# One pinned order for the first batch of an attention and gated-MLP kernel

## The chip, the cores and the metric

The kernel runs on one core of one Trainium2 chip. The time is the device time of one launch in microseconds (us); the median of several launches counts. Five engines work side by side, each through its own queue in order: TensorE (PE, matrix products), VectorE (DVE), ScalarE (ACT), GpSimd (POOL) and SyncE (SP), which here only issues DMA transfers between device memory and the on-chip memory. Engines wait for one another by semaphores.

## The reference: what is computed

Batch 8, 8 heads, sequence 576, head size 64, all in float32. Linear attention without a softmax comes first: per head a 64x64 product of keys and values, then queries times that product, then a normalization by the root mean square over the head. Its output, 512 columns wide, goes through an MLP with a spatial gate:

```
kv  = einsum('bhsd,bhse->bhde', k, v)
out = einsum('bhsd,bhde->bhse', q, kv)
x   = out / sqrt(mean(out*out) + 1e-6) * g_norm          # heads side by side: 512 columns
h   = relu(x @ w_in)                                     # 512 x 1024
u, v = h[..., :512], h[..., 512:]
v_n = (v - mean(v)) / sqrt(var(v) + 1e-6)
v_s = einsum('ts,bsd->btd', w_spatial, v_n) + b_spatial
return (u * v_s) @ w_out                                 # 512 x 512
```

The weights `w_in` and `w_out` reach the kernel as 64-bit numbers (two 32-bit words each) and are turned into float32 on the chip.

## The kernel before, in words

The 8 heads are taken as 4 pairs of 128 rows; the 576 positions are 4 tiles of 128 and a tail of 64. The batches are worked one after the other: `first(b)` (the v half, then the u half of the first MLP product), `second(b)` (the spatial product) and `last(b)` (the output product), with the attention of later batches put between their steps. From batch 1 on these products are made of three passes of a faster number format: each operand is split in a high and a low part (`WIH`, `WIL`, `XH`, `XL` and so on).

Batch 0 is different. Its weights are still arriving, so its products are made in plain float32 from the weights as they are decoded, and the splits of the weights are made meanwhile. What is done for batch 0, with the attention of batch 1 among it, is written as a string of tokens, `PLAN`, which a loop works through (lines 720 to 721). One letter is one step:

- `N`, `n`: zero products on PE whose result nobody reads (8, then four groups of 6, 8, 6 and 6 in the plan: the `n` groups are 26 in all).
- `W` issues the next weight load, `L` the next load of attention inputs. These come per pair: keys and values `KV` (128x1024 numbers) and their tail `KT`, then the queries `qt`. There are two buffers each.
- `C` decodes one weight tile: an absolute value on ACT (line 570) and five steps on DVE (lines 571 to 575).
- `J` is the key-value product of one pair, `K` that of two (line 128), with two copies of the result (lines 145 and 146).
- `A` and `D` are the product with the queries (line 203, and 156 for the tail's part) with the squares of the norm; `B` is the end of the norm on DVE; `T` is the transpose on PE (line 231) and its copy on ACT (line 233 for batch 0, 224 and 225 for others).
- `Hck` adds pair `k` to the v half of position tile `c` (line 366); it needs the transpose of pair `k` and the decoded tile `k` of `w_in`. `e` and `F` finish the v half. `ukj` is the same for the u half (line 390). `h` is the v half of the tails (line 372), `s` one unit of the spatial product in float32 (lines 399 and 400).
- `X`, `E`, `z` and `O` split weights for the batches to come (lines 579, 580, 623 to 631 and 319); `Q` decodes a tile of `w_out`; `R` splits the gated result `U` for the output product.

The tokens give the order in which instructions are recorded. A scheduler then puts each engine's instructions in an order of its own, by priorities and a model of times; only some instructions, marked by `keep_in_program_order`, stay in the recorded order among themselves. So the queue of an engine can differ from the plan. On SP a DMA also waits for the DMA eight places ahead of it, since eight semaphores go round.

Of batch 1, the loads of keys come first for all pairs and then all queries (line 634).

Of the kernel before, what the change touches and what calls it, by code (L numbers as in the profile page):

```python
# [10 lines left out]
U32 = mybir.dt.uint32  # L11
I32 = mybir.dt.int32
AF = mybir.ActivationFunctionType
ALU = mybir.AluOpType
# [3 lines left out]
DM, FF = 512, 1024  # L18
FH = FF // 2
P = 128  # L20
NP = H // 2
# [9 lines left out]
EPS = 1e-6  # L31
HALF = DM // 2
NB = B
PLAN = """
N8 W L J00 n6 D00 L n8 W G J01 n6 B00 C A01 L n6 W L J02 T00 H00 H10 D02 C H20 H30 B01 W C J03 T01 Z H01 H11 D03 H21 H31 W C
W B02 L T02 H02 H12 H22 H32 W B03 C W d0 T03 H03 H13 H23 H33 b0 e0 e1 e2 e3 C L C t0 L K10 C
u00 u01 u02 u03 F0 L F1 W W L K12 F2 W W W W d1 b1 F3 u10 Q0 u11 X0 u12 L A10 X1 u13 t1 X2 L B10 A11 h X3
T10 s L B11 E0 T11 s A12 s L B12 E1 z s T12 A13 X4 W s B13 L X5 Q1 s T13 X6 L s X7 s P O0 O1 p R W
"""


def f32(ap):
    return ap.bitcast(F32)
# [3 lines left out]
def body(ctx: ExitStack, tc, qT, kvm, kvt, g2, w_in, wsT, bsp, w_out, out):  # L47
    nc = tc.nc
# [5 lines left out]
    work = ctx.enter_context(tc.tile_pool(name="work", bufs=2))  # L54
# [23 lines left out]
    R = [vpool.tile([P, 14 * HF], F32, name=f"R{x}", tag=f"V{x}") for x in "HL"]  # L78
# [42 lines left out]
    def att_k(b, pairs, st, copy=nc.vector.tensor_copy):  # L121
        ps = ps_att.tile([P, 512], F32, name="pskv", tag="att")
        to = KVO[pairs[0] // 2] if b % 2 else KVB
        ends, first = [], None

        def product(p, of, h, c):
            at = (p - pairs[0]) * P + h
            return nc.tensor.matmul(ps[h:h + D, at:at + D], of[:, 0, h:h + D], of[:, 1, h:h + D],  # L128
                                    start=c == 0, stop=c == NC)

        for p in reversed(pairs):
            kv, kt, qs = keys.pop((b, p))
# [12 lines left out]
        copy(to[0:D, own, 0:D], both[0:D, :, 0:D])  # L145
        nc.scalar.copy(to[D:P, own, D:P], both[D:P, :, D:P])
        for p, qs in reversed(ends):
            if qs is not None:
                att_end(p, st, qs)
        issue()  # L150

    def att_end(p, st, q):

        if p == 0:
            st["tail"] = ps_tail.tile([P, 512], F32, name="pst", tag="tail")
        nc.tensor.matmul(st["tail"][:, p * P:(p + 1) * P], q, st[p], start=True, stop=True)  # L156
# [42 lines left out]
    def att_qa(b, p, st, accumulate=False):  # L199
        qt = queries.pop((b, p))  # L200
        ps = ps_att.tile([P, 512], F32, name="pso", tag="att")
        for c in range(NC):
            nc.tensor.matmul(ps[:, c * P:(c + 1) * P], qt[:, c * P:(c + 1) * P], st[p],  # L203
                             start=True, stop=True)
        if b % 2 == 0:
            att_end(p, st, qt[:, S - P:S])
        issue()
        st[p] = norm_a(ps, P, accumulate)
# [330 lines left out]
    staged, decoded, psu = {}, {}, {}  # L539
# [20 lines left out]
    def load_out(k):  # L560
        load64(w_out[k * P:(k + 1) * P, :], 2 * NP + k, stage0 if k == 1 else stage2)

    def weight64(i):

        wide = staged.pop(i).rearrange("p (f two) -> p f two", two=2)
        w0, w1 = wide[:, :, 0], wide[:, :, 1]
        to = W32[i] if i < 2 * NP else f32(w1)
        t = work.tile([P, DM], U32, name="t", tag="stg", bufs=2)
        keep = tc.keep_in_program_order if i in (2 * NP, 2 * NP + 1) else lambda ins: ins
        keep(nc.scalar.activation(f32(t), f32(w1), AF.Abs, scale=2.0 ** -112))  # L570
        keep(nc.vector.tensor_scalar(t, t, 3, None, op0=ALU.logical_shift_left))
        nc.vector.scalar_tensor_tensor(w1, w1, 0x80000000, t, op0=ALU.bitwise_and, op1=ALU.bitwise_or)
        nc.vector.tensor_scalar(t, w1, 0xFF800000, None, op0=ALU.bitwise_and)
        nc.vector.scalar_tensor_tensor(f32(w0), w0, 2.0 ** -52, f32(t), op0=ALU.mult, op1=ALU.mult)
        nc.vector.tensor_tensor(to, f32(w1), f32(w0), op=ALU.add)
        return to
# [7 lines left out]
        split_w(WIH[:, n % NP, fs], WIL[:, n % NP, fs], W32[n])  # L584

    def make_out(k):
        decoded[k] = weight64(2 * NP + k)

    def split_out(k):
        split(WOH[:, k, :], WOL[:, k, :], decoded.pop(k))  # L590
# [41 lines left out]

    todo = [(0, p, "f") for p in range(NP)]
    for b in range(1, B):
        kinds = ("k", range(NP)), ("q", range(NP))
        if b % 2 == 0:
            kinds = [(kind, ps) for ps in ((0, 1), (2, 3)) for kind in "eq"]
        todo += [(b, p, kind) for kind, ps in kinds for p in ps]
    states = {}
    wanted = [0]  # L640
# [7 lines left out]
    def ahead(n=1):  # L648
        wanted[0] += n
        issue()  # L650
# [11 lines left out]
    def warm(n):  # L662

        ps = ps_tail.tile([P, 512], F32, name="psw", tag="tail")
        for _ in range(n):
            nc.tensor.matmul(ps[:, 0:P], KVB[:, 1], KVB[:, 1], start=True, stop=True)

    def filler(n):
        for _ in range(n):
# [5 lines left out]
    def enqueue(b, late=0):  # L675
        if b < NB:
            queue.extend(att_steps(b)[late])
# [12 lines left out]
    def outw():  # L690
# [5 lines left out]
    loads = [lambda k=k: load_in(1, k) for k in range(NP)]  # L696
    loads += [lambda k=k: load_in(0, k) for k in range(NP)]
    loads += [lambda c=c: load_ws(c) for c in range(NC)] + [load_tail]
    loads += [lambda k=k: load_out(k) for k in range(NP)]
    makes = list(range(2 * NP))  # L700
    units = [(d, j) for d in range(4) for j in range(2)]

    psv = [ps_mm.tile([P, 512], F32, name="psh", tag="mm") for _ in range(NC)]
    st = [states.setdefault(b, {}) for b in range(2)]
    do = {
        "N": warm, "n": filler,
        "L": lambda: ahead(), "W": lambda: loads.pop(0)(), "C": lambda: weight64(makes.pop(0)),
        "K": lambda b, p: att_k(b, (p, p + 1), st[b]), "A": lambda b, p: att_qa(b, p, st[b]),
        "B": lambda b, p: att_qb(b, p, st[b]), "T": lambda b, p: att_t(b, p, st[b]),
        "J": lambda b, p: att_k(b, (p,), st[b], nc.scalar.copy),  # L710
        "D": lambda b, p: att_qa(b, p, st[b], True), "d": lambda b: tail_a(b, st[b], True),
        "a": lambda b: tail_a(b, st[b]), "b": lambda b: tail_b(b, st[b]),
        "t": lambda b: att_tail(b, st[b]),
# [3 lines left out]
        "s": lambda: sp_32(*units.pop(0)), "X": split_in, "E": split_ws, "z": split_tail,  # L717
        "Z": blank_tails, "P": outw, "p": gates, "Q": make_out, "O": split_out, "R": split_g,
    }
    for token in PLAN.split():  # L720
        do[token[0]](*map(int, token[1:]))

    ahead(len(todo))
    VH, VL = (vpool.tile([P, 2, 7, HF], F32R, name=f"V{x}", tag=f"V{x}") for x in "HL")
# [35 lines left out]
    last(1)  # L760
    for b in range(2, NB):
        first(b)
# [50 lines left out]
```

## Time and profile before

| | us |
|---|---|
| median of 3 runs (lowest, highest) | 522.61 (522.24, 522.8) |
| the profiled execution's own time | 521.54 |
| its span, first to last instruction | 519.7 |
| PE busy | 507.7 (98% of the span) |
| DVE busy | 360.0 (69%) |
| ACT busy | 240.1 (46%) |

The span is read from the first to the last instruction of the profiled execution. A busy PE is one with a matmul in flight. A float32 matmul of the program counts as two in the trace's numbers (x8 for four steps). The DMA engines are busy all the time from 8 to 29 us (share 1.02), and at 0.82 from there to 40 us; after that they have room.

### The profile page before, as it was taken

What the parts mean: (1) busy time and instruction counts of PE and PEld (TensorE: products, weight loads), DVE (VectorE), ACT (ScalarE), POOL (GpSimd) and SP (SyncE); (2) the same over time, 40 slices, a digit from 0 to 9 for tenths busy, and PEclk for the clock granted to TensorE, in tenths of its full rate; (3) what the DMA queues carried; (4) which work ended last, traced back from release to release, by engine and by line L of the source; (5) the groups of instructions that cost most, each with busy time, mean ns of one, the idle gap of its engine ahead of it and who ended that gap; (6) DMA issues with size and microseconds to landing.
All of it is one profiled execution on the core that took longest, in us unless ns stands there. A gap on an engine that the chain in (4) does not pass through costs nothing.

```text
span 519.7 us, 9439 instructions
## 1 busy us (share of the span) xinstructions
PE 507.7 (98%) x3548; PEld 450.0 (87%) x3548; DVE 360.0 (69%) x1075; ACT 240.1 (46%) x615; POOL 8.5 (2%) x23
## 2 busy tenths in 40 slices
PE   7889999999999999999999999999999999999996
PEld 7647878798998899889998899989998899988995
DVE  3987498998781788648593598918785388938470
ACT  3554565674533464335343356325443355434321
POOL 5000000000000000000000000000000000000000
PEclk9999999999999999999999999999999999999999
DMA  8985110333326002111425401230233201020003
GB/s 267 346 309 170 56 45 23 93 126 90 124 96 197 12 2 64 41 65 53 139 79 172 133 22 33 75 133 3 76 101 133 73 1 34 9 82 0 1 1 101
DMA packets 22304, 46.50 MB, mean 89 GB/s; under 512 B 2866, under 2 KB 7474, under 8 KB 22260
## 3 DMA queue, kind: packets, MB, share of 16 engines
q1 hardware_dynamic: 22260, 45.91, 27.3%
q8 instruction: 28, 0.46, 0.3%
q14 instruction: 16, 0.13, 0.1%
HBM read 36.46 MB, written 9.44 MB: 88 GB/s over the span
## 4 chain that ended last, share of the span: by engine, by line
PE 86%; DMA 5%; DVE 4%; ACT 3%; issue 1%; SPq 0%; DVEq 0%
PE pso L283 19%; PE psu L283 17%; PE psh L316 13%; PE psb L422 6%; PE pso L203 4%; PE psc L422 4%; PE psa L422 4%; PE pskv L128 4%; DMA KV<-kvm 3%; PE psu L390 3%; PE pstr L231 2%; PE psh L366 2%; PE psh L283 2%; PE pst L156 1%; DMA KT<-kvt 1%; DVE WSL L580 1%
## 5 line engine op out<-in xcount | busy, mean ns | idle before, releaser
L283 PE MATMUL psu<-XH,WIH 128*128 128x288 f32 x224 | 66.5, 297 | 0.0
L283 PE MATMUL psu<-XL,WIH 128*128 128x288 f32 x224 | 66.1, 295 | 0.0
L283 PE MATMUL psu<-XH,WIL 128*128 128x288 f32 x224 | 66.0, 295 | 0.0
L283 PE MATMUL pso<-WOH,GH 128*128 128x512 f32 x144 | 57.1, 398 | 0.0
L283 PE MATMUL pso<-WOL,GH 128*128 128x512 f32 x144 | 56.7, 394 | 0.0
L283 PE MATMUL pso<-WOH,GL 128*128 128x512 f32 x144 | 54.0, 396 | 0.0
L449 ACT CAST GH<-g 128x288 fp32r<-128x288 f32 (+2 forms) x84 | 26.7, 350 | 47.9 <-DVE g L441 47.5
L295 DVE BATCH_NORM_STATS2 s<-v 128x6 f32<-128x512 f32 x32 | 22.0, 691 | 36.2 <-ACT v L289 36.1
L316 PE MATMUL psh<-WIH,XH 128*128 128x512 f32 x112 | 44.3, 396 | 0.0
L316 PE MATMUL psh<-WIL,XH 128*128 128x512 f32 x112 | 43.7, 390 | 0.0
L316 PE MATMUL psh<-WIH,XL 128*128 128x512 f32 x112 | 43.0, 391 | 0.1
L283 PEld LDWEIGHTS psu<-XH,WIH 128*128 128x128 f32 x224 | 42.0, 188 | 0.4
L283 PEld LDWEIGHTS psu<-XL,WIH 128*128 128x128 f32 x224 | 42.0, 188 | 0.3
L283 PEld LDWEIGHTS psu<-XH,WIL 128*128 128x128 f32 x224 | 42.0, 188 | 0.0
L320 DVE TENSOR_TENSOR VL<-v,VH 128x512 fp32r<-128x512 f32 (+1 forms) x56 | 33.8, 621 | 7.9 <-ACT VH L319 7.6
L523 ACT COPY o<-pso 128x512 f32<-128x512 f32 x35 | 19.7, 588 | 39.6 <-PE pso L283 28.6
L190 DVE TENSOR_REDUCE ss<-x 128x8 f32<-128x512 f32 x35 | 23.8, 681 | 19.1 <-ACT x L189 19.0
L413 ACT ACTIVATE U<-psu 128x288 f32<-128x288 f32 x56 | 22.9, 412 | 28.5 <-PE psu L283 27.5
L319 ACT CAST VH<-v 128x512 fp32r<-128x512 f32 (+1 forms) x56 | 30.4, 564 | 10.8 <-DVE v L342 7.0
L283 PEld LDWEIGHTS pso<-WOH,GL 128*128 128x128 f32 x144 | 27.0, 188 | 5.7
L283 PEld LDWEIGHTS pso<-WOL,GH 128*128 128x128 f32 x144 | 27.1, 188 | 5.0
L283 PEld LDWEIGHTS pso<-WOH,GH 128*128 128x128 f32 x144 | 27.1, 188 | 4.7
(187 smaller groups left out, 1219.1 us busy)
## 6 DMA issues: line engine op xcount, KB each, us to landing
KV<-kvm SPq DMA_DIRECT2D x31, 512.0 KB, 4.4
out<-o SPq DMA_DIRECT2D x32, 256.0 KB, 2.1
qt<-qT SPq DMA_DIRECT2D x16, 288.0 KB, 2.9
stage<-w_in SPq DMA_DIRECT2D x8, 512.0 KB, 9.0
qt<-qT SPq DMA_DIRECT2D x16, 256.0 KB, 2.7
KT<-kvt SPq DMA_DIRECT2D x32, 64.0 KB, 4.1
stage<-w_out SPq DMA_DIRECT2D x4, 512.0 KB, 4.4
stage<-wsT SPq DMA_DIRECT2D x4, 288.0 KB, 5.2
```

What stands on the lines that cost most here:

```text
L128: return nc.tensor.matmul(ps[h:h + D, at:at + D], of[:, 0, h:h + D], of[:, 1, h:h + D], start=c == 0, stop=c == NC)
L190: nc.vector.tensor_reduce(ss, heads(x), axis=AX.X, op=ALU.add)
L203: nc.tensor.matmul(ps[:, c * P:(c + 1) * P], qt[:, c * P:(c + 1) * P], st[p], start=True, stop=True)
L283: nc.tensor.matmul(ps, lt, rh, start=i == 0, stop=i == n - 1)
L295: nc.vector.bn_stats(s6, v)
L316: nc.tensor.matmul(ps, lt, rh, start=k == 0 and i == 0, stop=k == NP - 1 and i == 2)
L319: nc.scalar.copy(hi, x)
L320: nc.vector.tensor_tensor(lo, x, f32(hi), op=ALU.subtract)
L413: nc.scalar.activation(U[:, d, cols], ps[:, 0:HS], AF.Relu)
L422: nc.tensor.matmul(ps, lt, rh, start=start and i == 0, stop=stop and i == len(pairs) - 1, skip_group_check=True)
L449: nc.scalar.copy(GH[:, d, dst], g[:, src])
L523: nc.scalar.copy(o, ps)
```

## The change

The plan is written anew. Three kinds of marks are in it: a stretch in brackets is pinned, which means that its instructions on PE, ACT and SP keep their recorded order (DVE's don't); a bar makes everything recorded after it stand behind the last DVE instruction recorded before it; and a new letter `c` is the first half of a decode (ACT's absolute value), with `C` the rest on DVE. 6 zero products of the 26 are left. The copies of `K` are both on ACT. The loads of batch 1 come in two halves: keys of two pairs, their queries, then the other two. The two decodes of `w_out` in the plan are pinned as well.

```diff
-N8 W L J00 n6 D00 L n8 W G J01 n6 B00 C A01 L n6 W L J02 T00 H00 H10 D02 C H20 H30 B01 W C J03 T01 Z H01 H11 D03 H21 H31 W C
...
+[ W N8 G L c W C J00 L A00 c C L L n6 W J01 A01 J02 B00 T00 | W D02 B01 c H00 H20 J03 H30 T01 A03 C B02 W H31
+W c T02 c c H21 H10 W H22 H11 H32 C B03 c C H01 W T03 H02 | H12 H33 c H03 L H13 H23 e0 L L W C C L a0 C e1 ]
...
-    def weight64(i):
+    def weight64_a(i):
...
+        t = work.tile([P, DM], U32, name="t", tag="stg", bufs=2)
+        nc.scalar.activation(f32(t), f32(w1), AF.Abs, scale=2.0 ** -112)
+        staged[i] = w0, w1, t
+
+    def weight64_b(i):
+        w0, w1, t = staged.pop(i)
...
     def make_out(k):
-        decoded[k] = weight64(2 * NP + k)
+        pin = pinned() if k < 2 else None
+        weight64_a(2 * NP + k)
+        decoded[k] = weight64_b(2 * NP + k)
+        if pin:
+            pin()
...
-        kinds = ("k", range(NP)), ("q", range(NP))
-        if b % 2 == 0:
-            kinds = [(kind, ps) for ps in ((0, 1), (2, 3)) for kind in "eq"]
+        keyed = "k" if b % 2 else "e"
+        kinds = (keyed, range(NP)), ("q", range(NP))
+        if b % 2 == 0 or b == 1:
+            kinds = [(kind, ps) for ps in ((0, 1), (2, 3)) for kind in (keyed, "q")]
...
+    def pinned():
+
+        traced = nc.cur_bb.bb.instructions
+        start = len(traced)
+
+        def end():
+            last = {}
+            for ins in list(traced[start:]):
+                if ins.engine in PINNED:
+                    if ins.engine in last:
+                        tc.add_manual_dep(
+                            ins, last[ins.engine].name,
+                            mybir.DependencyInfo(mybir.DependencyClass.NoSync,
+                                                 mybir.DependencyReason.DATA), reason="order")
+                    last[ins.engine] = ins
+
+        return end
...
-        "K": lambda b, p: att_k(b, (p, p + 1), st[b]), "A": lambda b, p: att_qa(b, p, st[b]),
+        "c": lambda: weight64_a(makes[0].pop(0)),
+        "C": lambda: weight64_b(makes[1].pop(0)),
+        "K": lambda b, p: att_k(b, (p, p + 1), st[b], nc.scalar.copy), "A": lambda b, p: att_qa(b, p, st[b]),
...
+    hold = behind = None
     for token in PLAN.split():
-        do[token[0]](*map(int, token[1:]))
+        if token in "[]":
+            hold = pinned() if token == "[" else hold()
+        elif token == "|":
+            behind = next(i for i in reversed(nc.cur_bb.bb.instructions)
+                          if i.engine == mybir.EngineType.DVE)
+        else:
+            with tc.issue_after(behind) if behind else ExitStack():
+                do[token[0]](*map(int, token[1:]))
```

On PE, in the middle of batch 0's v half (`pskv` is a key-value product, `pstr` a transpose, `pso` and `pst` the product with the queries, `psh` the v half), before:

```order
L366 MATMUL psh<-RL,RH 128x512 x4
L128 MATMUL pskv<-KV_99 64x64 x8
L128 MATMUL pskv<-KT_101 64x64 x2
L231 MATMUL pstr<-ident,x 128x128 x4
L366 MATMUL psh<-RL,RH 128x512 x4
L203 MATMUL pso<-KVB,qt 128x128 x4
L156 MATMUL pst<-KVB,qt 128x128
L231 MATMUL pstr<-ident,x 128x128 x4
L366 MATMUL psh<-RL,RH 128x512 x4
L231 MATMUL pstr<-ident,x 128x128 x4
L241 MATMUL pstt<-ident,x 128x128 x4
L128 MATMUL pskv<-KV_99 64x64 x8
```

and in the changed kernel:

```order
L367 MATMUL psh<-RL,RH 128x512 x2
L129 MATMUL pskv<-KV_99 64x64 x8
L129 MATMUL pskv<-KT_101 64x64 x2
L367 MATMUL psh<-RL,RH 128x512
L232 MATMUL pstr<-ident,x 128x128 x4
L204 MATMUL pso<-KVB,qt 128x128 x4
L157 MATMUL pst<-KVB,qt 128x128
L367 MATMUL psh<-RL,RH 128x512
L232 MATMUL pstr<-ident,x 128x128 x4
L367 MATMUL psh<-RL,RH 128x512 x6
L232 MATMUL pstr<-ident,x 128x128 x4
L367 MATMUL psh<-RL,RH 128x512 x2
```

The first-product steps stand in fours before and in twos, ones and a six now. Behind the last row shown stand, in the changed kernel, the key-value products of batch 1's first two pairs and the last four first-product steps.

On ACT, at the second pair of batch 0 (`t<-stage` is the absolute value of a decode, `KVB` the copies of a key-value product, `x` the squares and `sh` the root of a norm, `RH` the copy of a transpose), before:

```order
L570 ACTIVATE t<-stage 128x512
L145 COPY KVB<-pskv 64x64
L146 COPY KVB<-pskv 64x64
L570 ACTIVATE t<-stage 128x512
L189 ACTIVATE x<-pso 128x512
L570 ACTIVATE t<-stage 128x512
L165 ACTIVATE sh<-ss,epsc 128x8
L145 COPY KVB<-pskv 64x64
L146 COPY KVB<-pskv 64x64
L233 ACTIVATE RH<-pstr,gcol 128x512
```

and in the changed kernel:

```order
L569 ACTIVATE t<-stage 128x512
L146 COPY KVB<-pskv 64x64
L147 COPY KVB<-pskv 64x64
L190 ACTIVATE x<-pso 128x512
L166 ACTIVATE sh<-ss,epsc 128x8
L146 COPY KVB<-pskv 64x64
L147 COPY KVB<-pskv 64x64
L234 ACTIVATE RH<-pstr,gcol 128x512
```

Two decodes have moved from between the copies to later; the root of the second pair's norm still stands ahead of the third pair's copies.

On ACT again, near the end of the plan (`WTH` and `WTL` are the split of the spatial weights' tail, `XH` the copy of a batch-1 transpose, `v` the v half of batch 1, `GH` the split of the gated result), before:

```order
L579 CAST WSH<-stage 128x288 x7
L623 CAST WTH<-WT_118 64x576
L625 CAST WTH<-WT_118 64x576
L627 CAST WTL_81<-WT_118 1x576 x2
L224 ACTIVATE XH<-pstr,gcol 128x512
L189 ACTIVATE x<-pso 128x512
L629 CAST WTL_82<-WTL_81 64x576
L631 CAST WTL_82<-WTL_81 1x576
L319 CAST WOH<-stage 128x512
L631 CAST WTL_82<-WTL_81 1x576
```

and in the changed kernel:

```order
L225 ACTIVATE XH<-pstr,gcol 128x512
L631 CAST WTH<-WT_118 64x576
L633 CAST WTH<-WT_118 64x576
L635 CAST WTL_81<-WT_118 1x576 x2
L637 CAST WTL_82<-WTL_81 64x576
L147 COPY KVB<-pskv 64x2x64
L639 CAST WTL_82<-WTL_81 1x576
L290 ACTIVATE v<-psh 128x512 x2
L639 CAST WTL_82<-WTL_81 1x576
L320 CAST GH<-U 128x576 x4
```

The seven casts of the tail's split stood ahead of the copy of batch 1's third transpose before; now they stand behind that of the fourth and last one, directly ahead of the v half of batch 1.

On SP, in the changed kernel, the loads of batch 0's four pairs stand ahead of five of the eight `w_in` tiles; before, seven `w_in` tiles stood ahead of the fourth pair's keys. The small `gcol` (128 numbers) is now the second DMA instead of the tenth.

## Rows read from the trace of the kernel before

**Rows 1.** The page, part 1: busy us, share of the span, instructions.

```profile
PE 507.7 (98%) x3548; PEld 450.0 (87%) x3548; DVE 360.0 (69%) x1075; ACT 240.1 (46%) x615; POOL 8.5 (2%) x23
```

**Rows 2.** Busy by stretch: length, PE, PEld, DVE, ACT, POOL, clock, DMA share, GB/s.

```profile
8.17:28.80 20.63, 17.58 (x160) 13.98 (x161) 16.29 (x44) 11.56 (x53) 0.14 (x1) 1.00 1.02 338
28.80:40.00 11.20, 9.31 (x47) 5.27 (x47) 8.85 (x24) 6.00 (x38) 0.00 (x0) 1.00 0.82 285
...
64.89:102.80 37.91, 37.91 (x204) 29.28 (x202) 33.47 (x84) 23.80 (x48) 0.00 (x0) 1.00 0.17 51
```

**Rows 3.** PE's timeline: start, us, what, in brackets the idle time before.

```profile
1.06 3.78 PE L666 MATMUL psw<-KVB 128*128 128x128 f32 x16 [1.06 <-DVE epsc L653]
...
8.06 1.60 PE L671 MATMUL psh<-KVB 128*128 128x128 f32 x12
...
34.88 3.70 PE L366 MATMUL psh<-RL,RH 128*128 128x512 f32 x8 [1.76 <-ACT RH L233]
```

**Rows 4.** The chain that ended last, in order of time: start, us, what.

```profile
1.92 5.38 DMA KV<-kvm
...
14.57 11.00 DMA KV<-kvm
...
31.57 0.91 PE pso L203 x8
...
38.59 0.44 PE pstr L231 x4
...
39.78 1.31 PE pskv L128 x40
41.09 3.63 PE psh L366 x8
...
54.89 1.46 PE psu L390 x6
...
106.45 12.72 PE psu L283 x96
```

**Rows 5.** ACT's timeline, squares, root and copy in front.

```profile
16.37 0.60 ACT L189 ACTIVATE x<-pso 128x512 f32<-128x512 f32 x1
...
17.89 0.30 ACT L165 ACTIVATE sh<-ss,epsc 128x8 f32<-128x8 f32 x1 [0.26 <-DVE ss L190]
...
18.67 0.21 ACT L145 COPY KVB<-pskv 64x64 f32<-64x64 f32 x1 [0.48 <-PE pskv L128]
```

**Rows 6.** DVE's timeline: decode and norm in front, then rows of batch 1.

```profile
16.84 0.42 DVE L571 TENSOR_SCALAR t<-t 128x512 uint32<-128x512 uint32 x1
17.17 0.68 DVE L190 TENSOR_REDUCE ss<-x 128x8 f32<-128x512 f32 x1
17.77 0.68 DVE L572 SCALAR_TENSOR_TENSOR stage<-stage,t 128x512 uint32<-128x512 uint32 x1
...
57.89 0.69 DVE L195 TENSOR_TENSOR x<-pst,rh 128x512 f32<-128x512 f32 x1
...
60.92 0.69 DVE L195 TENSOR_TENSOR x<-pso,rh 128x512 f32<-128x512 f32 x1
64.89 0.48 DVE L225 SCALAR_TENSOR_TENSOR XL<-pstt,gcol,XH 128x256 fp32r<-128x256 f32 x1 [3.27 <-PE pso L203]
...
90.57 0.76 DVE L628 TENSOR_TENSOR WTL<-WT,WTL 1x576 fp32r<-1x576 f32 x1 [1.40 <-ACT WTL L627]
...
102.07 0.75 DVE L225 SCALAR_TENSOR_TENSOR XL<-pstr,gcol,XH 128x512 fp32r<-128x512 f32 x1
```

**Rows 7.** ACT's timeline around the start of batch 1's products.

```profile
87.72 0.67 ACT L623 CAST WTH<-WT 64x576 fp32r<-64x576 f32 x1
...
99.49 0.69 ACT L224 ACTIVATE XH<-pstr,gcol 128x512 fp32r<-128x512 f32 x1 [0.88 <-PE pstr L231]
...
103.92 1.57 ACT L289 ACTIVATE v<-psh 128x512 f32<-128x512 f32 x3
...
105.93 2.42 ACT L319 CAST GH<-U 128x576 fp32r<-128x576 f32 x4
```

More of the change, by code (lines that the diff above doesn't have):

```diff
@@ L33 @@
 NB = B
+PINNED = (mybir.EngineType.PE, mybir.EngineType.Activation, mybir.EngineType.SP)
 PLAN = """
-N8 W L J00 n6 D00 L n8 W G J01 n6 B00 C A01 L n6 W L J02 T00 H00 H10 D02 C H20 H30 B01 W C J03 T01 Z H01 H11 D03 H21 H31 W C
-W B02 L T02 H02 H12 H22 H32 W B03 C W d0 T03 H03 H13 H23 H33 b0 e0 e1 e2 e3 C L C t0 L K10 C
-u00 u01 u02 u03 F0 L F1 W W L K12 F2 W W W W d1 b1 F3 u10 Q0 u11 X0 u12 L A10 X1 u13 t1 X2 L B10 A11 h X3
-T10 s L B11 E0 T11 s A12 s L B12 E1 z s T12 A13 X4 W s B13 L X5 Q1 s T13 X6 L s X7 s P O0 O1 p R W
+[ W N8 G L c W C J00 L A00 c C L L n6 W J01 A01 J02 B00 T00 | W D02 B01 c H00 H20 J03 H30 T01 A03 C B02 W H31
+W c T02 c c H21 H10 W H22 H11 H32 C B03 c C H01 W T03 H02 | H12 H33 c H03 L H13 H23 e0 L L W C C L a0 C e1 ]
+e2 e3 W F1 u00 L F2 u01 K10 Z L F0 A10 b0 t0 L F3 u02 u03 K12 u10 d1 b1 B10 A11 | u11 t1 L u12 W | W W W A12
+X2 Q0 h X3 u13 s s B12 T10 E0 s s B11 X0 E1 A13 s s X1 X5 W B13 T12 T11 s X7 Q1 s T13 z P O1 p X4 X6 O0 W R
 """
@@ L561, in load_out @@
         load64(w_out[k * P:(k + 1) * P, :], 2 * NP + k, stage0 if k == 1 else stage2)
-    def weight64(i):
+    def weight64_a(i):
         wide = staged.pop(i).rearrange("p (f two) -> p f two", two=2)
         w0, w1 = wide[:, :, 0], wide[:, :, 1]
+        t = work.tile([P, DM], U32, name="t", tag="stg", bufs=2)
[3 more added lines that the diff above has]
+        w0, w1, t = staged.pop(i)
         to = W32[i] if i < 2 * NP else f32(w1)
[L568 to L571, printed above, removed]
+        nc.vector.tensor_scalar(t, t, 3, None, op0=ALU.logical_shift_left)
         nc.vector.scalar_tensor_tensor(w1, w1, 0x80000000, t, op0=ALU.bitwise_and, op1=ALU.bitwise_or)
@@ L699, in body @@
     loads += [lambda k=k: load_out(k) for k in range(NP)]
-    makes = list(range(2 * NP))
+    makes = [list(range(2 * NP)) for _ in range(2)]
     units = [(d, j) for d in range(4) for j in range(2)]
@@ L706, in body @@
         "N": warm, "n": filler,
-        "L": lambda: ahead(), "W": lambda: loads.pop(0)(), "C": lambda: weight64(makes.pop(0)),
-        "K": lambda b, p: att_k(b, (p, p + 1), st[b]), "A": lambda b, p: att_qa(b, p, st[b]),
+        "L": lambda: ahead(), "W": lambda: loads.pop(0)(), "c": lambda: weight64_a(makes[0].pop(0)),
+        "C": lambda: weight64_b(makes[1].pop(0)),
+        "K": lambda b, p: att_k(b, (p, p + 1), st[b], nc.scalar.copy), "A": lambda b, p: att_qa(b, p, st[b]),
         "B": lambda b, p: att_qb(b, p, st[b]), "T": lambda b, p: att_t(b, p, st[b]),
```

## The prediction

> **What bounds the kernel now.** I read the page's first part, then the stretches, PE's timeline, and last the chain. PE is busy for 507.7 of 519.7 us [rows 1]. So the program lasts as long as PE's work does, and only the 12 us in which PE had nothing to do, and the zero products, can be won. By stretches they lie in front: PE is busy for 17.58 of 20.63 us up to 28.8, for 9.31 of 11.20 up to 40 [rows 2], and in the stretch from 64.89 to 102.80 for all of it. What ends the waits in front is seen in the chain: it runs through two transfers of keys that end at 7.30 and at 25.57, and from about 35 on through PE alone [rows 4]. The last wait of size is 1.76 us for the copy of a transpose [rows 3]. DMA is busy throughout that stretch (share 1.02) [rows 2], so what stands ahead of the fourth pair's keys in the queue decides when they come.
>
> The reader is to see a second thing in the stretches: between 64.89 and 102.80 DVE is busy for 33.47 of 37.91 us [rows 2]. A PE that arrives there some us earlier finds a DVE that has only 4.4 us to give.
>
> **The front, step by step.** Loads first. Between the two key transfers of the chain [rows 4] there landed, by the order of SP's queue, nine pieces of 512 KB, three of 288 and four of 64 (sizes by shape, four bytes a number): 5728 KB in 18.27 us, or 313 KB per us. In the new order the fourth pair's keys and tail have 3824 KB between them and the first keys (five of 512, three of 288, four of 64, one of 144): 12.2 us. I add 0.2 us to the first keys for `gcol`, now ahead of them (an estimate), so 7.5 + 12.2 = 19.7 us, against 25.57 before. The second pair of batch 1, which `K10` needs, has 7888 KB: 25.2 us, so 32.7.
>
> The Trainium skill (DMA: Bandwidth & Descriptors, Specifications) gives a limit of some 358 GB/s per core for device memory. The stretch's 338 GB/s lies below it [rows 2]; at the skill's figure `K10` would have its data at 30.1, an estimate from that page, and the gain below would be 0.6 larger.
>
> Then the start of the third pair's product `D02`, which hangs on the norms. `J00` ends near 8.3. Two copies take 0.42, the product 0.91, squares 0.60, the sum on DVE 0.68, the root 0.30 [rows 4 to 6]: 11.3. ACT then makes the second decode's absolute value (0.6, as the squares of the same shape), and DVE has 0.42 + 0.68 + 0.69 + 0.42 + 0.68 of decode and norm ahead of the second pair's sum (0.68) [rows 6]: 15.5. Its root (0.30) stands in ACT's queue ahead of the third pair's two copies (0.42), as the order shows: 16.2, and 16.6 with some 0.04 for each hand-over. PE idles there for about 1.3 us.
>
> From 16.6 on PE has work in a row. One `D02` and one `A03` at 0.91 + 0.22, sixteen first-product steps at 3.63 / 4 = 0.91, `J03` 0.65, `K10` 1.31, three transposes at 0.44 [rows 4]: 2.3 + 14.5 + 0.65 + 1.3 + 1.3 = 20.0 us. `J03` is reached at 19.5 and waits 0.2. The copy of the third transpose stands behind a decode on ACT, 0.3. `K10` is reached at 32.1 and waits 0.6 for its data. The fourth tile is decoded by 30.1 (three and a half decodes of 2.9 and two norms behind 16.6 on DVE), its transpose copied by 32.0; both come before they are wanted at 34. So the last first-product step ends at 16.6 + 20.0 + 1.0 = 37.6. Before, it ended at 41.09 + 3.63 = 44.7, with one step more done by then: the tail's transpose, 0.7 between the chain's rows [rows 4]. **The front gains 44.7 - 37.6 - 0.7 = 6.4 us.** The 20 zero products that go are not counted besides: they filled waits, and their 0.13 us each [rows 3] is in that difference.
>
> **What is given back.** Behind 38 the same PE work follows (u half, spatial product, batch 1), PE without a wait as before if the others keep up.
>
> DVE: its norm of batch 1's first pair ended at 61.6 [rows 6]. In the new order it stands right behind the norm of batch 1's tail, and that waits for a product which PE reaches after a product with queries, 23 u steps, `K12`, two tail steps and one more product with queries: 37.6 + 0.9 + 23 x 0.49 + 1.3 + 1.1 + 0.9 = 53.1 [rows 4], and 0.4 for itself. Before, such a norm ended 3.7 after its product (54.9 to 58.6) [rows 4, 6]; with 0.6 for the second one that makes 57.8. From 61.6 to the split of the last transpose (ended at 102.8) DVE took 41.2 us, with a wait of 3.27 in front that goes [rows 6]. Four weight splits and one of `w_out`, 0.6 each, are now done earlier than before, 3.0 more; the tail weights' two splits with a wait of 1.40 [rows 6] come later, 2.9 less. So 57.8 + 41.2 - 3.3 + 3.0 - 2.9 = 95.8, or 7.0 earlier than before. PE asks for 6.4. That fits by 0.6 us; I take two waits for DVE of 0.2 each, at a freed bank and at the last weight split that the v half needs, since queues that meet so closely do not mesh.
>
> ACT: the seven casts of the tail weights at 0.67 [rows 7] stood well ahead of batch 1's v half and now stand between the last transpose's copy and the v tiles. That copy ended at 100.2 [rows 7] and ends at 94.2, by 6.4 - 0.4. Six casts and a key-value copy follow, 4.2: 98.4. Then two v tiles 1.05, the seventh cast 0.67, four splits of the gated result 2.42, a v tile 0.52, a decode's start 0.6, two squares 1.2, small roots 0.6 and the first copy of `U` 0.4 [rows 5, 7]: 105.9. PE starts the u half at 106.45 - 6.0 = 100.4 [rows 4] and has four banks; its fourth unit begins after 36 of the 96 matmuls of 12.72 [rows 4], at 105.2, and needs that first bank again. It waits 0.7. With 0.3 for the key-value copy, late in the same queue, I take 1.0 on ACT. **Given back: 1.4 us**, from 0 (ACT gets there sooner) to 3.3 (DVE keeps its old wait).
>
> From the output product of batch 0 on I cost the new order at nothing: PE is the bound there, and DVE and ACT have room (69% and 46% over the span) [rows 1]. The fourth `w_out` tile is decoded some 4 us later against PE's place than before; PE's order has all products with that tile behind the other three tiles', which covers it. Without that cover it would cost those 4 us.
>
> **Sum.** 6.4 - 1.4 = 5.0 us. Against the profiled execution: 521.54 - 5.0 = 516.5. That execution lies 1.07 under the median of the runs shown, so in medians 522.61 - 5.0 = **517.6 us**.
>
> **Bounds.** The load rate is the largest unknown. At the stretch's 338 GB/s (330 KB per us) `K10` has its data at 31.4 and waits for nothing; at the 285 GB/s of the next stretch [rows 2], 278 KB per us, at 35.9, and 3.2 more us are lost. I take 313, measured over the very pieces that move. With the give-back's 0 to 3.3 the gain runs from 0 (6.4 - 3.2 - 3.3) to 7.0.
>
> **Rivals.**
> - *The gain ends at DVE and ACT.* The queues of 57 to 106 us don't follow PE, and 3 us are given back more. For it: 33.47 of 37.91 us busy, and a queue in fixed order cannot use its gaps. Against it: the waits there ended with PE, which comes sooner. Gain 2.0 to 3.0, about 520.2.
> - *The loads come late.* Five `w_in` tiles in a row stand ahead of batch 1's first keys, and a pinned PE cannot go round `K10`. For it: 285 GB/s between 28.8 and 40. Against it: there the queue wasn't full (share 0.82), since transfers waited for buffers; now eight are always out. Gain 1.8, about 520.8.
> - *Nothing is given back.* 6.4 to 7.0, about 515.8.
> - *The clock falls (slower).* The first sixteen zero products take 3.78 us, 0.24 each; twelve later ones 1.60, 0.13 each [rows 3]: half pace at 1.2 GHz against 2.4. The zero products that go were what kept PE busy between the first pairs; from 8.3 to 16.6 it idles 3.5 us now in waits of 0.4 to 1.3. If the clock falls there and stays down over the dense part, each us of PE work costs one more. From 5.0 us of such work on it decides; over `D02` and eight first-product steps it would be 8.4, so 526.0. Against it: from 28.8 to 40 PE idled 1.9 of 11.2 us at a granted 1.00 [rows 2], with one wait of 1.76, longer than any of the new ones.
>
> By the Trainium skill (TensorE: Matmul & The Clock Gate, What's actually happening) the lower clock is the default and activity releases it, which is a rule against taking zero products away. The trace agrees on the start (0.24 against 0.13 us); the front without the zero products is shown by no row of before.
>
> That the change doesn't do what it says can be left out: the order of the built program shows the pinned rows as written.
>
> **Chances.** The forecast, 516.4 to 518.8: 0.50. Nothing given back: 0.14. DVE and ACT: 0.15. Late loads: 0.10. The clock: 0.06. Others: 0.05. The range that leaves out no more than 2 in 10 reaches from 515.3 (a gain of 7.3, the bound and a little of run to run) to 521.0 (the late loads). Faster by over 0.2% (1 us, about what a measurement of this kernel can tell from no change) is all of the first two and nearly all of the next two: 0.87. Slower: the clock and half of the others, 0.08. Same: 0.05.
>
> **What would show it.** Each step has its row in the changed kernel's profile: the fourth pair's key-value product near 19.7 on PE, the third pair's query product at 16.6, the last first-product row (`psh`, L367) ending at 37.6 with a wait of about half a us before `K10` that a DMA ends. The granted clock must be 1.00 in front, and the first-product rows 0.45 us apart. The split of the last transpose on DVE should end near 96, and batch 1's u half start near 100, with one wait for ACT's `U` behind it. The forecast is wrong if `K10`'s data come after 34, if DVE's row comes later than 98, if first-product rows stand 0.9 us apart, or if PE shows waits of over a us behind 115, where I cost nothing.

## The result, and the profile after

The changed kernel takes 517.55 us (median of 5 runs, 517.0 to 518.5), the kernel before 522.35 on the same chip (522.19 to 522.8). The ratio is 0.9908, interval 0.9893 to 0.9922: a gain of 4.8 us, between 4.1 and 5.6. The forecast was 517.6 and a gain of 5.0. The execution profiled after the change took 517.55 us with a span of 515.8, so between the two profiled executions the gain is 4.0 us (3.9 of span); the sums below are made on these.

Part 1 of the page, and the busy time by stretch (length, PE, PEld, DVE, ACT, POOL, clock, DMA share, GB/s), the second and third stretch as in [rows 2]:

```profile
PE 505.7 (98%) x3508; PEld 447.5 (87%) x3508; DVE 359.9 (70%) x1076; ACT 236.4 (46%) x572; POOL 8.5 (2%) x23
```

```profile
8.00:13.00 5.00, 4.40 (x29) 4.22 (x26) 1.75 (x4) 1.44 (x5) 0.27 (x1) 1.00 1.01 363
...
8.17:28.80 20.63, 18.85 (x147) 13.84 (x144) 14.71 (x41) 10.47 (x38) 0.10 (x1) 1.00 1.02 345
28.80:40.00 11.20, 11.20 (x74) 6.34 (x74) 11.16 (x26) 6.12 (x13) 0.00 (x0) 1.00 0.98 306
60.00:97.91 37.91, 37.24 (x196) 28.53 (x197) 35.47 (x89) 20.83 (x46) 0.00 (x0) 1.00 0.09 28
```

In those two stretches PE was busy for 26.89 us before, now for 30.05, with 40 zero matmuls fewer in the program. In the last, of the same length as the third one shown before, DVE has 2.4 us left instead of 4.4, and PE waits there, which it did not.

PE's timeline after (start, us, what, in brackets the idle time before):

```profile
9.10 2.08 PE L204 MATMUL pso<-KVB,qt 128*128 128x128 f32 x8 [0.60 <-ACT KVB L147]
11.40 2.18 PE L698 MATMUL psh<-KVB 128*128 128x128 f32 x12
13.51 0.69 PE L129 MATMUL pskv<-KV 128*64 128x64 f32 x16
...
18.06 1.16 PE L204 MATMUL pso<-KVB,qt 128*128 128x128 f32 x8 [0.53 <-ACT KVB L147]
...
21.09 0.69 PE L129 MATMUL pskv<-KV 128*64 128x64 f32 x16
...
33.44 0.69 PE L129 MATMUL pskv<-KV 128*64 128x64 f32 x16
...
34.75 3.70 PE L367 MATMUL psh<-RL,RH 128*128 128x512 f32 x8
...
75.40 2.21 PE L400 MATMUL psa<-stage,V 128*128 128x288 f32 x8 [0.58 <-DVE U L402]
...
101.58 0.38 PE L284 MATMUL psu<-XH,WIH 128*128 128x288 f32 x1
...
106.95 0.40 PE L284 MATMUL psu<-XH,WIH 128*128 128x288 f32 x1 [0.36 <-ACT U L414]
...
115.02 0.40 PE L284 MATMUL pso<-WOH,GH 128*128 128x512 f32 x1
```

And of the kernel before, the fourth pair's key product, and the two rows that answer to the third last and the last shown above:

```profile
25.71 0.69 PE L128 MATMUL pskv<-KV 128*64 128x64 f32 x16 [1.74 <-DMA KV<-kvm]
...
106.20 0.38 PE L283 MATMUL psu<-XH,WIH 128*128 128x288 f32 x1
...
119.01 0.40 PE L283 MATMUL pso<-WOH,GH 128*128 128x512 f32 x1
```

The reader is to see: the fourth pair's keys no longer hold PE (21.09, no wait listed; 1.74 before), nor does a transpose's copy (1.76 in [rows 3]). Two new waits of 0.58 and 0.36 us stand further back. Batch 1's u half, the same 96 matmuls, takes 115.02 - 101.58 = 13.44 us, where it took 12.81. From the output product at 115.02 to the end it is 400.8 us, before 400.7: nothing more is won or lost there.

So the gain falls out as 44.7 - 38.4 = 6.3 us at the last first-product row, less 0.7 for the tail's transpose done later: 5.6. Given back are 0.58 and a restart of 0.1 (the row behind it takes 2.21 instead of 2.10), a wait of 0.16 at 60.09, and 0.63 in the u half: 1.5. That leaves 4.1, where the spans differ by 3.9.

### The profile page after: what moved, and what is told of

Read it like the earlier page. It is cut to its first block, busy times and chain, and to the rows that moved or that the text cites. A ratio compares the mean times of both kernels' runs of the same rounds, so it can differ in the third digit from the quotient of the medians.

```text
span 515.8 us, 9316 instructions
## 1 busy us (share of the span) xinstructions
PE 505.7 (98%) x3508; PEld 447.5 (87%) x3508; DVE 359.9 (70%) x1076; ACT 236.4 (46%) x572; POOL 8.5 (2%) x23
## 4 chain that ended last, share of the span: by engine, by line
PE 91%; DMA 3%; ACT 3%; DVE 2%; issue 1%; SPq 0%; ACTq 0%
PE pso L284 19%; PE psu L284 16%; PE psh L317 14%; PE psb L423 6%; PE pso L204 5%; PE psc L423 4%; PE psa L423 4%; PE pskv L129 4%; PE psu L391 3%; PE pstr L232 2%; PE psa L400 2%; DMA stage<-w_in 2%; PE psh L367 2%; PE psh L284 2%; PE pst L157 1%; DMA KV<-kvm 1%
## 5 line engine op out<-in xcount | busy, mean ns | idle before, releaser
L191 DVE TENSOR_REDUCE ss<-x 128x8 f32<-128x512 f32 x38 | 25.9, 683 | 18.4 <-ACT x L190 18.2
L524 ACT COPY o<-pso 128x512 f32<-128x512 f32 x35 | 19.7, 589 | 35.1 <-PE pso L284 27.8
```

What stands on the lines that cost most here:

```text
L191: nc.vector.tensor_reduce(ss, heads(x), axis=AX.X, op=ALU.add)
L524: nc.scalar.copy(o, ps)
```

## Experiments

Each ran against the kernel before on its chip. The ratio of the change itself is 0.9908; in 522 us, 0.001 is half a us. My theory to begin with: the order of the loads makes the gain, since what PE waited for in front was keys.

**The old loads under the new order.**

```diff
-[ W N8 G L c W C J00 L A00 c C L L n6 W J01 A01 J02 B00 T00 | W D02 ...
+[ W N8 G L c W C J00 L W A00 c C L W W W W n6 J01 A01 J02 B00 L T00 | D02 ...
```

(three W further on are taken out for it)

> The changed kernel with one thing put back: seven w_in tiles stand on SP's queue ahead of the fourth pair's keys, as before the change (three were ahead of them in the changed kernel). PE's and DVE's order stay as they are, word for word. Theory (the gain is the load order; the PE order only makes it usable): the fourth keys land about 4.9 us later (three tiles of 512 KB at 313 KB per us), at 25.5 instead of 20.5; J03 waits 4.4 us for them and everything pinned behind it shifts; the last first-product row ends near 42.6 instead of 38.4 and the time is about 521.5, 4.0 over the changed kernel's 517.55. Rival (the gain is the new order of PE's stages and the zero products that went, the loads only follow): under 1.5 us is lost, 519 or less.

523.25 us, ratio 0.9998 (0.9984 to 1.0011): the whole gain is lost. PE's timeline in it:

```profile
25.39 0.69 PE L129 MATMUL pskv<-KV 128*64 128x64 f32 x16 [4.28 <-DMA KV<-kvm]
...
26.12 2.06 PE L367 MATMUL psh<-RL,RH 128*128 128x512 f32 x2
...
40.33 3.70 PE L367 MATMUL psh<-RL,RH 128*128 128x512 f32 x8
```

The keys hold PE for 4.28 us, as computed, and two first-product matmuls behind that wait take 2.06 us where they take 1.13: behind the wait PE is at half pace (granted clock 0.50 from 26.2 to 29.5 us). The last row ends 5.6 later. The earlier loads are necessary under this order. Are they enough?

**The new loads under the old order.**

```diff
+PINNED = (mybir.EngineType.SP,)
-N8 W L J00 ... e0 e1 e2 e3 C L C t0 L K10 C
+[ N8 W L J00 ... e0 e1 e2 e3 ] C L C t0 L K10 C
```

> The kernel before the change with SP alone held in the order of its plan, so that three instead of seven w_in tiles stand ahead of the fourth pair's keys; PE, ACT and DVE stay free, zero products stay, nothing else of the change is in it. Theory (the load order is the gain): the fourth keys land near 21 instead of 25.6, the wait of 1.74 us for them goes, and the last first-product row ends 3 to 4 us earlier than 44.7; 2.5 to 3.5 us under the kernel before (the 20 zero products and the waits for transposes stay in it). Rival (the old order of PE cannot use earlier keys, since decodes and norms hold the first products): under 1 us. The first experiment showed the reverse: the old loads under the new order lose the whole gain.

522.58 us, ratio 0.9994 (0.9982 to 1.0007): no gain; my theory fell in its simple form. PE's timeline:

```profile
26.13 0.69 PE L128 MATMUL pskv<-KV 128*64 128x64 f32 x16
...
33.49 3.70 PE L366 MATMUL psh<-RL,RH 128*128 128x512 f32 x8 [0.78 <-ACT RH L233]
...
38.40 3.70 PE L366 MATMUL psh<-RL,RH 128*128 128x512 f32 x8 [0.78 <-ACT RH L233]
```

The fourth keys landed at 20.2 in this run, and PE came for them at 26.13 without a wait: zero products and eight first-product matmuls stood ahead. Then it waited twice for transposes' copies. With `K10` behind it now, the front was still some 0.8 us ahead of the kernel before when `K10` ended (43.8); a wait of 1.2 us for DVE at 64.05, which the kernel before has not, took that back.

**The zero products back in the changed kernel.**

```diff
-... J00 L A00 c C L L n6 W J01 A01 J02 B00 T00 ...
+... J00 n6 L A00 c C L L n8 W J01 n6 A01 J02 n6 B00 T00 ...
```

> The changed kernel with the zero products between the first pairs put back (6, 8, 6 and 6 instead of one group of 6: 40 matmuls more), at the places that the kernel before had them. Theory (they were filling, and cost what they overrun): 40 x 0.13 = 5.2 us of work into waits of 0.6, 0.5 and 0.5 us; the third pair's query product starts some 2 us later, near 20, of which the wait for K10's data gives back part; about 519 (1.5 over the changed kernel). Rival (they keep PE at full pace, which the changed kernel lacks in front): 517.0 or less.

520.07 us, ratio 0.9943 (0.9923 to 0.9964): 1.8 us of the gain lost.

```profile
8.05 2.76 PE L698 MATMUL psh<-KVB 128*128 128x128 f32 x12
10.65 1.06 PE L204 MATMUL pso<-KVB,qt 128*128 128x128 f32 x8
...
20.24 1.06 PE L204 MATMUL pso<-KVB,qt 128*128 128x128 f32 x8
```

The first query product runs at full pace behind them (1.06 against 2.08), which saves 1.0 us, but they take 2.76 for it. The third pair's query product comes at 20.24 instead of 18.06.

**Loads and zero products together, old order of stages.**

```diff
-[ N8 W L J00 n6 D00 L n8 W G J01 n6 B00 C A01 L n6 W L J02 ...
+[ N8 W L J00 D00 L n6 W G J01 B00 C A01 L W L J02 ...
```

> The kernel before with two parts of the change at once and without the third: SP held in the order of its plan (fourth keys behind three w_in tiles), and one group of 6 zero products left of the 26 between the first pairs. The old plan of the stages stays, and PE, ACT and DVE stay free. Loads alone gained nothing (ratio 0.9994): there PE came to the fourth keys only at 26.1, since some 8 us of zero products, the first ones at half pace, stood ahead. Theory (early keys and a PE that is free for them make the gain together; the rest of the new order adds little): the fourth pair's key product near 21, the last first-product row ends 3 to 4 us before 44.7, 2.5 to 4 us under the kernel before. Rival (without the new order of decodes and roots on ACT and DVE the transposes' copies come late, as the two waits of 0.78 and one of 1.2 in the loads-alone run): less than 1.5 us under it.

522.6 us, ratio 0.9988 (0.9972 to 1.0005). The time is as the rival said: much of PE's idle time turned into waits for ACT and DVE. The rows of the view of waits (us in total, times, longest), and the last first-product row:

```profile
PE pso L203 <- ACT KVB L146: 2.3, 3, 1.2
...
PE psh L366 <- ACT RH L233: 2.2, 3, 0.8
PE pstt L241 <- DVE qh L173: 1.2, 1, 1.2
PE psu L283 <- ACT v L289: 0.5, 1, 0.5
```

```profile
36.72 3.70 PE L366 MATMUL psh<-RL,RH 128*128 128x512 f32 x8 [0.78 <-ACT RH L233]
```

But the theory's sign came too: the last first-product row ended at 40.4, 4.3 us before 44.7. `K10` (1.3) and the tail's transpose (0.4) stand behind it here, so the front won some 2.5 us like for like. The last two rows of waits lie behind the front, at 62.37 and 103.43, and take back 1.7 of that. So the loads and fewer zero products do win time in front, and the old order behind loses most of it again. The part of the new plan behind the brackets was not run by itself.

**What has to be held: SP alone, or ACT too.** The changed kernel with fewer engines held in the plan's order:

```diff
-PINNED = (mybir.EngineType.PE, mybir.EngineType.Activation, mybir.EngineType.SP)
+PINNED = (mybir.EngineType.SP,)                              # first run
+PINNED = (mybir.EngineType.Activation, mybir.EngineType.SP)  # second run
```

> The changed kernel with SP alone held in the plan's order; PE and ACT are free in the front, as before the change. Theory (the order of the loads is what had to be held; PE's free order is nearly the same): within 0.2% of the changed kernel's ratio of 0.9908 to the kernel before. Rival (ACT's held order matters: free, it starts decodes ahead of roots and the last first products wait for transposes' copies): 1 to 2 us of the gain are lost, 0.993 to 0.995.

521.61 us, ratio 0.9976 (0.9959 to 0.9993): 3.6 us of the gain lost, more than the rival said. Its waits, and two rows of ACT's timeline:

```profile
PE pstr L232 <- DVE x L196: 2.2, 1, 2.2
PE psu L391 <- ACT V L742: 1.8, 1, 1.8
```

```profile
44.65 0.66 ACT L569 ACTIVATE t<-stage 128x512 f32<-128x512 f32 x1 [4.97 <-DMA stage<-w_out]
45.22 1.07 ACT L742 ACTIVATE V<-psh 128x512 f32<-128x512 f32 x2
```

ACT stood for 4.97 us before the start of a `w_out` decode whose load hadn't landed, and the copies of V, which PE needed, stood behind it. The kernel before kept the starts of these decodes in order by a mark (`keep`, line 569), which the change takes away; the pin that it puts there covers a single ACT instruction and so holds nothing. So this run frees more of ACT than the kernel before did, and about half of the loss hangs on that start. Holding ACT as well should bring it back:

> The changed kernel with ACT and SP held in the plan's order and only PE free. With SP alone held, the ratio to the kernel before was 0.9976 instead of 0.9908; in its trace PE waited 2.23 us for a transpose whose norm stood behind two decodes on DVE, and 1.81 us for a copy of V on ACT, which stood behind the start of a w_out decode that waited 4.97 us for its load. Theory (ACT's held order, which also sets when decodes reach DVE, is what is worth those 3.5 us): with ACT held the ratio is 0.990 to 0.992. Rival (PE's held order, the fourth pair's key product and the transposes among the first products, is worth it): 0.995 or more.

518.29 us, ratio 0.9908 (0.9886 to 0.9930): all of it. Holding PE adds nothing that shows; PE's free order ended its last first-product row at 39.2, after a third pair's query product that came 0.6 later in that run. What the bars, which hold back work behind DVE, are worth was not run by itself.

**The pace in front.** The first query product at half pace was not in my sum. Can more zero products at the start, where PE only waits, prevent it?

```diff
-[ W N8 G L
+[ W N8 N4 G L
```

> The changed kernel with twelve instead of eight zero products at the very start (24 instead of 16 matmuls), so that PE works on until the first keys land at 6.6. In the changed kernel's trace the first query product takes 2.08 us for 8 matmuls, in the kernel before 1.06: PE was still at half pace there. Theory (the late rise of the clock is part of why the third pair's query product came at 18.1 and not at 16.6): the first query product takes 1.06, the third pair's starts near 17, and as K10's data land at 33.1 and hold PE there, the last first-product row ends near 38.0: 0.4 us won, 517.1. Rival (the clock rises at its own time, whatever stands at the start): the first query product still takes over 1.5 us, no change. Second rival (the pair products are paced by their loads): full pace, but the third pair's product within 0.3 of 18.1, no change.

517.66 us, ratio 0.9900 (0.9877 to 0.9923): no change.

```profile
6.54 0.45 PE L129 MATMUL pskv<-KV 128*64 128x64 f32 x8
...
9.21 1.79 PE L204 MATMUL pso<-KVB,qt 128*128 128x128 f32 x8 [1.30 <-DMA qt<-qT]
...
18.02 1.16 PE L204 MATMUL pso<-KVB,qt 128*128 128x128 f32 x8 [0.19 <-ACT KVB L147]
```

The key product was at full pace (0.45), and after a wait of 1.30 the query product was slow again. So the first rival's sign came (over 1.5 us), but not for its reason: the clock had risen early and fell again, the granted clock being 0.50 from 9.5 to 12.9 us. The third pair's product came at 18.02, as the second rival had it.

**The second pair's keys earlier, then K10 later too.**

```diff
-[ W N8 G L c W C J00 L A00 c C L L n6 W J01
+[ W N8 G L L c W C J00 A00 c C L L W J01         # both runs
-H03 L H13 H23 e0 L L W ... F2 u01 K10 Z
+H03 L L H13 H23 K10 e0 L W ... F2 u01 Z          # second run only
```

> The changed kernel with the second pair's keys ahead of the second w_in tile and without its last group of zero products. In the changed kernel the third pair's query product starts at 18.06 whatever PE did before it (18.01 and 18.02 with old loads and with more zero products at the start), and the second pair's keys landed near 13.1. Theory (that product hangs on the second pair's keys through a norm): the keys land near 10.5, the second pair's product starts at 11.6, right behind the first pair's, and the third pair's query product near 16.5. The gain behind it is small, since the fourth keys (20.7) and K10's data (33.1) then hold PE: the last first-product row ends at 38.0 to 38.4, 0 to 0.5 us won. Rival (PE at half pace, or ACT, holds it): it starts within 0.4 us of 18.06.

518.09 us, ratio 0.9904 (0.9887 to 0.9922), no change. The keys landed at 10.8 and their product began at 11.87, yet the third pair's query product came at 18.81: PE was at half pace up to 19 in this execution. The column of the clock shows it (8 to 18 us, the number ahead of the last two):

```profile
8.00:18.00 10.00, 7.57 (x62) 6.81 (x62) 6.06 (x14) 3.15 (x9) 0.28 (x1) 0.55 0.94 317
```

> As the second-keys-first kernel, and the key product of batch 1's first two pairs (K10) is moved behind the last first-product step, so that PE no longer needs its data at 33. Theory (the front is then bound by its own work from the third pair's query product on): the last first-product row ends at 38.4 - 1.3 (K10, now behind it) - 0.5 to 1.0, so at 36.1 to 36.6, and 0.5 to 1.0 us of the whole time are won against the changed kernel. Rival (DVE's decodes bind there: the third and fourth w_in tile are decoded at 32.9 in the changed kernel): the row ends at 37.1 or later and nothing is won.

518.12 us, ratio 0.9906 (0.9889 to 0.9923), no change. In this run PE was back at full pace from the second pair's query product on, and it shows what holds the third pair's. PE, then DVE, then ACT:

```profile
13.42 1.16 PE L204 MATMUL pso<-KVB,qt 128*128 128x128 f32 x8 [0.90 <-ACT KVB L147]
...
17.64 1.16 PE L204 MATMUL pso<-KVB,qt 128*128 128x128 f32 x8 [1.52 <-ACT KVB L147]
```

```profile
15.64 0.69 DVE L578 SCALAR_TENSOR_TENSOR stage<-stage,t 128x512 f32<-128x512 uint32 x1
16.25 0.68 DVE L191 TENSOR_REDUCE ss<-x 128x8 f32<-128x512 f32 x1
```

```profile
14.61 0.60 ACT L190 ACTIVATE x<-pso 128x512 f32<-128x512 f32 x1 [1.25 <-PE pso L204]
16.96 0.30 ACT L166 ACTIVATE sh<-ss,epsc 128x8 f32<-128x8 f32 x1 [1.75 <-DVE ss L191]
```

The squares end at 15.2, the sum waits behind a decode's rows until 16.25, the root until 16.96, and the copies for the third pair stand behind the root. The second pair's key product came 2.3 us sooner than in the changed kernel (11.18 against 13.51) and made the third pair's query product 0.4 sooner. The last first-product row ended at 36.9, but the key product moved behind it takes 1.3, and PE then waited 0.60 at 49.83: nothing is left of it.

**What is given back: three tries to save it.** The tail's casts earlier on ACT, the first split of the spatial weights later, its sums on POOL:

```diff
-E1 A13 s s X1 X5 W B13 T12 T11 s X7 Q1 s T13 z P O1     # first run
+E1 A13 z s s X1 X5 W B13 T12 T11 s X7 Q1 s T13 P O1
-s s B12 T10 E0 s s B11 X0                               # second run
+s s B12 T10 s s B11 E0 X0
-nc.vector.tensor_tensor(x, b12, b11, op=ALU.subtract)   # third run, and three more like it
+nc.gpsimd.tensor_tensor(x, b12, b11, op=ALU.subtract)
```

> The changed kernel with the seven casts of the tail weights on ACT moved from behind the last transpose's copy to ahead of the last weight splits, about where the kernel before had them. Theory (these casts are the ACT term of what is given back): the wait of 0.36 us at the fourth unit of batch 1's u half, and the restart with it, goes: batch 1's u half runs 12.8 us instead of 13.4, 0.6 us won, 516.9. Rival (ACT's queue is full there in any order, since weight splits come later in exchange): the wait turns up at another place, within 0.3 of 517.55. Second rival (the weight splits become late for PE): 0.5 to 1.5 slower.

526.69 us, ratio 1.0068 (1.0043 to 1.0094). The second rival came, and far larger. Two waits are left in its view of waits that the changed kernel has not or has smaller:

```profile
PE psh L317 <- ACT WIH L583: 3.4, 1, 3.4
PE psu L284 <- ACT U L414: 2.4, 1, 2.4
```

They sum to 5.4 us over the 0.36 of the changed kernel. Behind the first of them PE is at half pace, four transposes take 1.05 us for 0.60. The granted clock was at half behind both waits (stretches of this run, columns as above):

```profile
93.20:96.50 3.30, 3.10 (x12) 2.28 (x14) 2.35 (x5) 2.37 (x6) 0.00 (x0) 0.50 0.00 0
113.70:117.00 3.30, 3.05 (x13) 3.06 (x14) 3.30 (x11) 1.37 (x5) 0.00 (x0) 0.50 0.01 2
```

PE was busy there for 3.10 and 3.05 us at half pace, work of half that time at full pace: 3.1 us lost. That is most of the other 3.6 us of span; 0.65 was lost in front already (last first-product row ended at 39.10 instead of 38.45).

> The changed kernel with the first split of the spatial weights (ten rows on DVE, five on ACT) moved from ahead of the seventh and eighth spatial unit to behind them. Theory (DVE is what holds the freed bank: its products of gate and tail stand behind these rows at 70 to 75): the wait of 0.58 us at the fifth unit and its restart go, 0.6 us won. Rival (DVE and ACT are full up to batch 1's products, and what is put off there comes out as a later wait, as with the tail weights' casts moved early): batch 1's first products wait for a weight split, 1 to 6 us slower.

519.91 us, ratio 0.9939 (0.9922 to 0.9957). The wait of 0.58 us is gone from the view of waits, and a longer one stands in its place:

```profile
PE psh L317 <- ACT WIH L583: 1.9, 1, 1.9
```

> The changed kernel with the eight sums of the spatial weights' split (128x288, 0.45 us each on DVE, 3.6 us together, between 70 and 91) given to POOL, which is idle there. Twice a piece of work put off on DVE or ACT between 70 and 106 came out as a later and longer wait. Theory (between 60 and 95 DVE is full, and only work taken off it helps): the wait of 0.58 us at the fifth spatial unit goes or shrinks and no new one comes, 0.5 to 1.0 us under the changed kernel, ratio near 0.989. Rival (a sum on POOL takes so long, or holds DVE up so much, that the weight splits behind it are late): batch 1's first products wait, 1 us or more slower.

518.05 us, ratio 0.9903 (0.9876 to 0.9931), nothing to tell from the changed kernel. The wait at the fifth unit shrank by 0.1 us only:

```profile
PE psa L400 <- DVE U L402: 0.5, 1, 0.5
```

A sum on POOL took 0.8 to 0.9 us. Less work on DVE did not bring the product that frees the bank forward, so its place in DVE's queue is the likelier reason; that was not tried by itself. The run before doesn't settle it: there a transpose stood on PE in the place of the wait (0.60 us at 75.29).

No version beat the changed kernel by more than the measurement can tell.

## Why the prediction was right

The size and the way were right: 5.0 forecast, 4.8 measured in medians, in both cases a front gain less a give-back. By the rows the gain is 4.1 only. The profiled execution of before lies 0.8 under its median (521.54 against 522.35), that of after at its own, so much of the closeness of 5.0 and 4.8 is luck. By its steps:

- *Loads.* The fourth keys and their tail were to be there at 19.7 and landed at 20.7; K10's data at 32.7, and they landed at 33.1. The rate behind that, 313 KB per us, was near; the pieces that PE waits for came somewhat later than their bytes alone say. `K10` found its data, since PE too came later, at 33.44 instead of 32.1.
- *The third pair's query product.* Forecast 16.6, measured 18.06. This is the term that was mis-sized. I put the first query product at the chain's 0.91, and it took 2.08, the tail's part 0.24 more and the zero products behind it 2.18 instead of 1.60. So the clock's rival was partly there, in a form I had not priced: PE did not fall back over dense work, it was at half pace in front (1.2 GHz) until 12 or 13 us. The sign that I had named for it, a granted clock of 1.00, stood in the column all the same (see the last section). The path was another one too. I let DVE's decode rows end last, and left out that the second pair's products stand behind the zero products on PE. In the trace DVE stood idle before the second pair's sum, until the squares that hang on these products were done:

```profile
16.66 0.69 DVE L191 TENSOR_REDUCE ss<-x 128x8 f32<-128x512 f32 x1 [0.39 <-ACT x L190]
```

  The run with K10 behind shows that DVE's decode alone would have held the product to 17.6. In exchange the waits of 0.2, 0.3 and 0.6 us that I had counted behind it (1.0 in the sum, though they add up to 1.1) did not come, and the work counted at 20.0 us took 20.4. So of 1.5 us of lateness 0.8 is left (a front gain of 5.6 instead of 6.4).
- *Zero products.* That they can go without loss is shown: back in place they cost 1.8 us, although in that run the query product behind them was at full pace.
- *Given back.* Forecast 0.4 on DVE at the freed bank and the weight splits and 1.0 on ACT; measured 0.58 and a restart at the bank, 0.16 at a copy, 0.63 in the u half: 1.5 for 1.4. By engine it was less even: 0.7 at DVE's bank against 0.4, and 0.8 behind ACT against 1.0. The last transpose's split on DVE was to end near 96 and did (DVE's timeline, then ACT's around the start of the u half):

```profile
95.68 0.75 DVE L226 SCALAR_TENSOR_TENSOR XL<-pstr,gcol,XH 128x512 fp32r<-128x512 f32 x1 [0.41 <-ACT XH L225]
```

```profile
101.11 0.67 ACT L639 CAST WTL<-WTL 1x576 fp32r<-1x576 f32 x1
101.80 2.39 ACT L320 CAST GH<-U 128x576 fp32r<-128x576 f32 x4
...
106.47 1.03 ACT L414 ACTIVATE U<-psu 128x288 f32<-128x288 f32 x3
```

On ACT the last cast of the tail weights stands ahead of the gated result's split, and `U`'s first copy, which PE's bank waits for, comes at 106.47; the forecast had it end at 105.9.

- *The chain of before.* I read it as PE alone from about 35 us on. From 64.0 to 102.8 it runs through ACT, DVE and a load of `w_out`, although PE is busy all that time; two of its rows:

```profile
94.49 3.43 DMA stage<-w_out
...
102.15 0.68 DVE XL L225
```

  So DVE and ACT were level with PE there before the change, and what is given back starts from that.

- *The rest at nothing.* Right: 400.8 against 400.7 us from 115.02 on, and no wait of PE is listed behind 106.95.
- *The reason for the gain.* I told the front as one sum and did not say which part carries it; the first experiment's theory said the loads. The runs say that the loads do not do it alone, nor the new order alone. Old loads lose all of the gain, and so do new loads under the old order, with and without the zero products. Of the new order it is ACT's that must be held: with ACT free 3.6 us are lost, with PE free nothing.

The three rivals that did not come: the loads were not late at `K10`; the give-back did not reach 3 us, but the runs that shifted work on ACT and DVE show how near it was; and it was not nothing.

The Trainium skill (TensorE: Matmul & The Clock Gate, What's actually happening) says that the lower clock is the default state. The rows agree with that: the first query product took 1.8 to 2.1 us in all eleven traces without zero products just before it, PE having waited 0.6 to 1.4 us there; of the three traces with zero products there it took 1.06 in two, and 1.92 in the third, where twelve of them took 2.93 us.

## What to carry to other kernels

When PE waits for loads in front, moving the loads is half of an edit: look what PE, ACT and DVE would do with the time, since here earlier transfers left nothing in the whole time until the queues behind them were in order too. In a queue of fixed order, ask of each instruction that waits for a transfer what stands behind it: one start of a decode held copies for 4.97 us. Where a helper is busy for nine tenths of a stretch (DVE here, 35.47 of 37.91 us; ACT for 20.83), a short wait of PE may be as cheap as it gets: of three tries to save 0.4 and 0.6 us by moving work, two cost 1.6 and 8 and one changed nothing.

## What the runs showed of the hardware

PE's pace falls behind shorter waits than I had thought of: in one run a key product at full pace (0.45 us) was followed, after a wait of 1.30, by a query product at 1.79. It does not always fall: before the change the row behind a wait of 1.76 is at full pace [rows 3].

Not all of the half pace in front is the change's doing. Behind the same sixteen zero products and a wait of 1.7 to 1.8 us, the first key product took 0.45 us in the profile before (at 6.51) and 0.69 in the one after (at 6.65), though nothing ahead of it on PE had changed.

The column of the granted clock is to be read with care. Between 8 and 13 us after the change it stood at 1.00 while the query product took 2.08 us instead of 1.06. The trace's list of granted clocks begins at 12.8 us in that execution, and the column counts the time ahead of its first entry as full. In the run that showed 0.55 over the same kind of rows the list begins at 5.6. The durations of rows of one shape tell the pace in either case.
